# Three tiles turned by DMA instead of TensorE in a mixer and MLP block, with other load order, groups and explicit order lists

## The chip, the cores and the metric

One core of one Trainium2 chip. The metric is the device time of one execution in microseconds (us); a kernel's time is the median of several runs. Engines: TensorE (PE; its weight loads are PEld in the profile), VectorE (DVE), ScalarE (ACT), GpSimd (POOL) and SyncE (SP), which issues nearly all DMAs.

## What is computed

x is 1 x 2048 x 512 in bf16, w1 and w2 are 512 x 512, w3 is 512 x 1792, w4 is 1792 x 512.

```python
h = _gelu(_layernorm(x, axis=-1) @ w1)
c = D // 4
g0 = jnp.pad(h[:, :, 0*c:1*c], ((0, 0), (1, 0), (0, 0)))[:, :S, :]
g1 = jnp.pad(h[:, :, 1*c:2*c], ((0, 0), (0, 1), (0, 0)))[:, 1:, :]
g2 = jnp.pad(h[:, :, 2*c:3*c], ((0, 0), (2, 0), (0, 0)))[:, :S, :]
g3 = jnp.pad(h[:, :, 3*c:   ], ((0, 0), (0, 2), (0, 0)))[:, 2:, :]
hs = jnp.concatenate([g0, g1, g2, g3], axis=-1) @ w2
x1 = x + hs
h2 = _gelu(_layernorm(x1, axis=-1) @ w3) @ w4
return x1 + h2
```

The four quarters of h are shifted along the tokens by 1, -1, 2 and -2 before w2, so a tile of the first residual (x1) needs h of its own tile and of both neighbours.

## The kernel before

The 2048 tokens are 16 tiles of 128. All weights and activations stay in SBUF. A tile passes these steps; t is the tile, q is t in layer 1 and 16 + t in layer 2:

- Load: `dma_x..` and `dma_w..` from SP (line 384 for x, 393 for weights), in the order of `LOADS`. w1, w2 and w4 come in halves a and b, w3 in one piece.
- Statistics: either bn_stats and bn_aggr on DVE (`bnst`, `bnag`, lines 432 and 434), or, for q in `STAT_ACT`, sums and sums of squares on ACT (`sum`, `ssq`, lines 411 and 416) with small DVE steps (`mean`, `msq`, `vpe`). `rstd` is a power on POOL (line 439).
- `norm` on DVE, ACT or POOL by the table `NORM` (lines 461, 470, 473; for ACT and POOL with a small step `nmr` first) writes the normalized tile into one of 16 slots of `xn_buf`.
- The turn, tokens to columns, into `xnT`. On PE: four transposes of 128 x 128 through PSUM and an eviction (`tp` and `ev`, lines 506 and 514; `ty` in the script takes a PSUM pair of the up buffers, `tp` a bank of the other PSUM buffer). Or by DMA: one transposing DMA for the whole tile (line 479), also named `tp`, issued on SP's queue. Which one a tile gets is decided by whether the script names it: tiles 0 to 7 of layer 1 are on PE, the other 24 turns are DMAs.
- `up1` (w1, line 642) in groups of tiles by `GROUPS`: weights are the stationary operand, so a group of n tiles is 16 matmuls of 128 n columns. Tile 0 is done the other way round (`rows`, line 544) and its GELU output is turned by PE (`th`, line 610). GELU on ACT (line 657) writes `hT`.
- `mix` (w2, line 697): four matmuls of 512 columns, one for each shifted quarter; DVE adds x to give x1 (`x1_`, line 713 or 709). The first mix is cut in two parts by which half of w2 comes first.
- Layer 2: statistics, norm and turn again, `up2` (w3, line 642) in blocks of a group, GELU, `down` (w4, line 731): 14 matmuls of 512 columns. DVE adds x1 (`res`, line 739) and SP writes out. The last tile's columns go in pieces of 256, 160 and 96 with the output DMA on ACT's queue.

PE warms up on nine matmuls of zeros while the first x tiles load. Two PSUM banks serve mix, down and some turns, three pairs of banks serve up and the other turns.

PE's order is the order of `SCRIPT`. The order of the other engines is made by a planner in `Program.order` and `place`: each operation has an assumed duration (`dur`), a due time worked back from PE's order, a hand-set bias, and a model of the DMA queue; DMA turns are put among the loads of SP's queue by it. `emit` then writes the instructions in that order with semaphore waits. Every engine works its list in order, and SP's DMAs are issued in order: a DMA turn whose norm is not done holds up those listed after it.

Of the kernel before, what the change touches and what calls it, by code (L numbers as in the profile page):

```python
# [6 lines left out]
P = 128  # L7
# [4 lines left out]
LN_EPS = 1e-5  # L12
ENGINES = ["sp", "act", "pe", "dve", "pool"]

class Op:


    def __init__(self, name, eng, fn, reads, writes, dur, queue):
        self.name, self.eng, self.fn = name, eng, fn
        self.reads, self.writes = list(reads), list(writes)  # L20
        self.dur, self.queue = dur, queue
        self.idx = 0
        self.descs = 8.0
        self.prio = 1e9
        self.first = None

class Program:

    HOP = {"pe": 200.0, "dve": 155.0, "act": 220.0, "pool": 120.0, "sp": 70.0}
    LOOK = {"dve": 300.0, "act": 300.0}
    DUE = 179877.0
    BEGIN = {"sp": 30.0, "act": 150.0, "pe": 400.0, "dve": 150.0, "pool": 450.0}
    ENTRY = 1900.0
    COLD, RESTART = 4300.0, 800.0
    RING = 150.0
    LAG = {"load": 750, "tp": 350}

    def __init__(self):  # L40
        self.ops = []
        self.lines = []

    def add(self, eng, name, fn, reads=(), writes=(), dur=100.0, queue=None):
        op = Op(name, eng, fn, reads, writes, dur, queue)
        op.idx = len(self.ops)
        self.ops.append(op)
        return op

    def line(self, names):  # L50

        self.lines.append(list(names))

    def order(self):
# [25 lines left out]
        order_only = set()  # L80
        for names in self.lines:
            for a, b in zip(names, names[1:]):
                assert named[a].eng == named[b].eng, (a, b)
                order_only.add((named[a].idx, named[b].idx))
        last = None
        pe_pos = 0
        for op in self.ops:
            if op.eng == "pe":
                if last is not None:
                    preds[op.idx].add(last.idx)  # L90
                last = op
                op.prio = pe_pos
                pe_pos += 1
        order_only = {(a, b) for a, b in order_only if a not in preds[b]}
        for a, b in order_only:
            preds[b].add(a)
        succs = [set() for _ in self.ops]
        for i, d in enumerate(preds):
            for j in d:
                succs[j].add(i)  # L100
        left = [len(s) for s in succs]
        stack = [i for i, n in enumerate(left) if n == 0]
        seen = 0
        while stack:
            i = stack.pop()
            seen += 1
            for j in preds[i]:
                if self.ops[j].eng != "pe":
                    self.ops[j].prio = min(self.ops[j].prio, self.ops[i].prio)
                left[j] -= 1  # L110
                if left[j] == 0:
                    stack.append(j)
        assert seen == len(self.ops), "cycle"
        if self.DUE:

# [37 lines left out]
    def place(self, succs, order_only):  # L153
# [9 lines left out]
        fed = {}  # L163
# [745 lines left out]
```

## Time and profile before

| | |
|---|---|
| median of 3 runs | 135.59 us (135.45 to 135.73) |
| span of the profiled execution, first to last instruction | 133.7 us |
| around the span (135.59 - 133.7) | 1.9 us |
| PE busy | 130.6 us, 98% of the span |
| ACT, DVE, POOL busy | 56.0, 50.9, 30.9 us |
| DMA turns | 24, median 2.5 us from issue to landing |
| w3, one load of 1792 KB | 10.9 us from issue to landing |
| PE transposes of x tiles (line 506) | 32 matmuls, 3.4 us busy |

Times in the trace count from the span's start. The chain that ended last follows the work back from the last instruction; a piece of it is a start, a length and what ran. Busy time of PE overlaps between neighbours, since matmuls are pipelined and their ends are modelled; lengths in the chain do not overlap. Landing is the time from a DMA's issue to its last semaphore update. A run of matmuls is sometimes shown with one record fewer than was issued.

### The profile page before, as it was taken

What the parts mean: (1) busy time and instruction counts of PE and PEld (TensorE: products, weight loads), DVE (VectorE), ACT (ScalarE), POOL (GpSimd) and SP (SyncE); (2) the same over time, 40 slices, a digit from 0 to 9 for tenths busy, and PEclk for the clock granted to TensorE, in tenths of its full rate; (3) what the DMA queues carried; (4) which work ended last, traced back from release to release, by engine and by line L of the source; (5) the groups of instructions that cost most, each with busy time, mean ns of one, the idle gap of its engine ahead of it and who ended that gap; (6) DMA issues with size and microseconds to landing.
All of it is one profiled execution on the core that took longest, in us unless ns stands there. A gap on an engine that the chain in (4) does not pass through costs nothing.

```text
span 133.7 us, 2004 instructions
## 1 busy us (share of the span) xinstructions
PE 130.6 (98%) x776; PEld 71.8 (54%) x789; DVE 50.9 (38%) x138; ACT 56.0 (42%) x89; POOL 30.9 (23%) x69
## 2 busy tenths in 40 slices
PE   8999999999999999999999999999999999999994
PEld 3488768874488444444444444444444444444464
DVE  1899998887550830052260003322220000232223
ACT  5699998858657155520025553000006663000000
POOL 2447567696544120012022003100000000000000
PEclk9999999999999999999999999999999999999999
DMA  4999966745442991002211000311111000111112
GB/s 134 329 349 401 237 150 95 83 89 107 98 99 49 295 329 40 0 0 43 77 42 39 0 0 0 78 39 44 39 42 37 0 0 0 39 44 39 39 39 78
DMA packets 21305, 12.19 MB, mean 91 GB/s; under 512 B 13872, under 2 KB 20784, under 8 KB 21296
## 3 DMA queue, kind: packets, MB, share of 16 engines
q1 hardware_dynamic: 20864, 11.93, 32.7%
q10 hardware_dynamic: 432, 0.13, 0.4%
q8 instruction: 6, 0.10, 0.3%
q14 instruction: 3, 0.02, 0.1%
HBM read 6.82 MB, written 2.10 MB: 67 GB/s over the span
## 4 chain that ended last, share of the span: by engine, by line
PE 94%; DMA 2%; DVE 2%; issue 1%; SPq 0%
PE y_ps L642 46%; PE o_ps L731 36%; PE o_ps L697 10%; DMA x_sb<-in_x_dram 2%; PE y_ps L506 1%; DVE st L432 1%; PE y_ps L544 1%; DVE xn_buf L448 0%; DVE xn_buf L461 0%; DVE o_sb L739 0%; PE o_ps L610 0%; DVE mv L434 0%; SPq L894 0%
## 5 line engine op out<-in xcount | busy, mean ns | idle before, releaser
L642 PE MATMUL y_ps<-xnT,w_sb 128*128 128x512 bf16 (+2 forms) x421 | 63.6, 308 | 0.2
L642 PEld LDWEIGHTS y_ps<-xnT,w_sb 128*128 128x128 bf16 x424 | 38.4, 98 | 24.6 <-DVE mv L434 0.2
L731 PE MATMUL o_ps<-w_sb,h2T 128*128 128x512 bf16 (+3 forms) x248 | 48.7, 355 | 0.2
L657 ACT ACTIVATE h2T<-y_ps 128x1024 bf16<-128x1024 f32 (+1 forms) x29 | 28.6, 993 | 47.2 <-PE y_ps L642 47.1
L731 PEld LDWEIGHTS o_ps<-w_sb,h2T 128*128 128x128 bf16 x252 | 23.6, 98 | 25.2
L739 DVE TENSOR_TENSOR o_sb<-o_ps,x_sb 128x512 bf16<-128x512 f32 (+3 forms) x18 | 11.4, 632 | 45.7 <-PE o_ps L731 45.7
L439 POOL TENSOR_TENSOR rstd<-mv,neghalf 128x1 f32<-128x1 f32 x20 | 11.1, 553 | 35.1 <-DVE mv L434 30.1
L697 PE MATMUL o_ps<-w_sb,hT 128*128 128x512 bf16 x58 | 14.8, 379 | 0.3
L432 DVE BATCH_NORM_STATS2 st<-x_sb 128x6 f32<-128x512 bf16 x20 | 13.5, 676 | 2.6 <-DMA x_sb<-in_x_dram 2.5
L713 DVE TENSOR_TENSOR x_sb<-o_ps,x_sb 128x512 bf16<-128x512 f32 x10 | 6.8, 677 | 14.8 <-PE o_ps L697 14.8
L439 POOL TENSOR_TENSOR rstd<-vpe,neghalf 128x1 f32<-128x1 f32 x12 | 6.7, 558 | 15.6 <-DVE vpe L428 15.5
L473 POOL TENSOR_SCALAR xn_buf<-x_sb,rstd,nmr 128x512 bf16<-128x512 bf16 x12 | 9.2, 764 | 1.0 <-DVE nmr L466 0.4
L657 ACT ACTIVATE hT<-y_ps 128x512 bf16<-128x512 f32 (+1 forms) x10 | 8.1, 806 | 3.1 <-PE y_ps L642 2.9
L697 PEld LDWEIGHTS o_ps<-w_sb,hT 128*128 128x128 bf16 x64 | 6.1, 98 | 5.7
L709 DVE SCALAR_TENSOR_TENSOR x_sb<-o_ps,x_sb 128x512 bf16<-128x512 f32 x6 | 4.1, 681 | 12.1 <-PE o_ps L697 12.1
L416 ACT ACTIVATE junk<-x_sb 128x512 bf16<-128x512 bf16 x12 | 7.5, 622 | 2.1 <-DVE x_sb L709 2.0
L461 DVE TENSOR_SCALAR xn_buf<-x_sb,mv,rstd 128x512 bf16<-128x512 bf16 x13 | 6.1, 471 | 2.7 <-POOL rstd L439 2.0
L470 ACT ACTIVATE xn_buf<-x_sb,nmr,rstd 128x512 bf16<-128x512 bf16 x6 | 4.9, 813 | 0.5 <-POOL nmr L466 0.4
L756 PE MATMUL o_ps<-zeros 128*128 128x512 bf16 x9 | 4.0, 631 | 0.4 <-DVE zeros L363 0.4
L411 ACT ACTIVATE junk<-x_sb 128x512 bf16<-128x512 bf16 x6 | 3.7, 624 | 1.2 <-DMA x_sb<-in_x_dram 1.2
L434 DVE BATCH_NORM_AGGREGATE mv<-st 128x2 f32<-128x9 f32 x20 | 3.8, 192 | 0.3
L506 PE MATMUL y_ps<-ident,xn_buf 128*128 128x128 bf16 x32 | 3.4, 236 | 0.2 <-DVE xn_buf L461 0.2
(34 smaller groups left out, 28.7 us busy)
## 6 DMA issues: line engine op xcount, KB each, us to landing
out_dram<-o_sb SPq DMA_DIRECT2D x15, 128.0 KB, 1.7
w_sb<-in_w_dram SPq DMA_DIRECT2D x1, 1792.0 KB, 10.9
w_sb<-in_w_dram SPq DMA_DIRECT2D x2, 896.0 KB, 6.2
x_sb<-in_x_dram SPq DMA_DIRECT2D x4, 256.0 KB, 3.6
w_sb<-in_w_dram SPq DMA_DIRECT2D x4, 256.0 KB, 4.3
x_sb<-in_x_dram SPq DMA_DIRECT2D x5, 128.0 KB, 4.5
x_sb<-in_x_dram SPq DMA_DIRECT2D x1, 384.0 KB, 5.7
xnT<-xn_buf SPq DMA_TRANSPOSE x24, 2.5
```

The source lines that it names most:

```text
L416: (lambda d: (lambda e: e.activation(d, src, ACT_F.Square, accum_out=sums[:, q, 1:2])))(junk[:, b, :]),
L432: pg.add("dve", f"bnst{q}", lambda e: e.bn_stats(st9[:, q, 0:6], src), reads=rs, writes=[(("st", q), 0)], dur=605)
L439: lambda e: e.tensor_tensor(col(rstd), var, neghalf[:], ALU.pow),
L461: lambda e: e.tensor_scalar(dst, src, mv[:, q, 0:1], rstd[:, q : q + 1], ALU.subtract, ALU.mult),
L470: f = lambda e: e.activation(dst, src, ACT_F.Identity, bias=nmr[:, q : q + 1], scale=rstd[:, q : q + 1])
L473: f = lambda e: e.tensor_scalar(dst, src, rstd[:, q : q + 1], nmr[:, q : q + 1], ALU.mult, ALU.add)
L642: ins = e.matmul(y_ps[:, p, W * i : W * (i + 1)], wsb[:, dc, P * fc : P * (fc + 1)], src[:, dc, P * t0 : P * t0 + W], start=(dc == 0), sto ...
L657: (lambda d, s: (lambda e: e.activation(d, s, ACT_F.Gelu_apprx_tanh)))(dst, ysrc),
L697: ins = e.matmul(dst, hT[:, j, c0 : c0 + P], w2_sb[:, j, :], start=(j == order[0]), stop=(j == order[-1]))
L713: f = lambda e: e.tensor_tensor(x1_sb[:, t, :], dst, x_sb[:, t, :], ALU.add)
L731: ins = e.matmul(dst, h2T[:, fc, P * t : P * (t + 1)], w4_sb[:, fc, cs], start=(fc == 0), stop=(fc == FC - 1))
L739: (lambda d, c: (lambda e: e.tensor_tensor(o_sb[:, oi, c], d, x1_sb[:, t, c], ALU.add)))(dst, cs),
```

## The change

- Tiles 5, 6 and 7 of layer 1 are no longer in the script as turns, so they become transposing DMAs on SP's queue (tp5, tp6, tp7). PE turns tiles 0 to 4; tile 3 goes through the other PSUM buffer.
- Layer 1's groups: tiles 0 to 7 one by one (5 and 6 were a pair), then 2, 2 and 4. Layer 2's groups: 2, 4, 4, 4, 2 instead of 2, 2, 4, 4, 4.
- Loads: x5 alone between the halves of w1; x4 alone; x6 and x7 together, ahead of w2a; x8 and x9 together; w3 in four pieces of 448 KB (s, p, q, r), with tp5 between the second and the third; x10 to x15 and w4 on SP's queue after ten more DMA turns.
- The script names up2 blocks one at a time and mixes them with mix, down and up1.
- The planner is gone. `ORDER` lists every operation of SP, ACT, DVE and POOL; `order` only merges these lists and PE's script.
- Other tables of who does which statistics, norm and eviction: two tiles of layer 1 have their statistics on ACT instead of six; the eviction of tile 0's turned GELU output goes from DVE to ACT, tile 1's turn is evicted by ACT alone.

```diff
-GROUPS = {1: (1, 1, 1, 1, 1, 2, 1, 2, 2, 4), 2: (2, 2, 4, 4, 4)}
+GROUPS = {1: (1, 1, 1, 1, 1, 1, 1, 1, 2, 2, 4), 2: (2, 4, 4, 4, 2)}
-NORM = {5: "act", 6: "pool", 7: "act", 9: "pool", 10: "pool", 11: "act", 12: "act", 15: "pool", 18: "act", 19: "pool", 20: "act", 21: "pool", 23: "pool", 25: "pool", 26: "pool", 28: "pool", 30: "pool", 31: "pool"}
+NORM = {4: "act", 6: "act", 7: "pool", 10: "pool", 11: "act", 12: "pool", 14: "act", 16: "pool", 17: "pool", 18: "act", 20: "act", 21: "pool", 24: "act", 26: "pool", 27: "pool", 28: "pool", 29: "pool", 30: "act", 31: "act"}
-EVAC = {1: "both", 2: "dve", 4: "dve", 5: "dve", 6: "both", 7: "dve", 8: "dve", 9: "dve", ...
+EVAC = {0: "act", 1: "act", 2: "both", 3: "dve", 4: "both"}
-STAT_ACT = (0, 5, 7, 9, 10, 12, 19, 21, 23, 24, 25, 31)
+STAT_ACT = (0, 9, 18, 19, 23, 25, 26, 31)
...
-HEV = {0: "dve", 1: "dve", 2: "dve", 3: "dve", 4: "dve", 5: "dve", 6: "dve"}
-BIAS = {"bnag16": -989.166, "nmr10": 207.118, "rstd14": 756.261, "rstd5": 886.138, ...
+HEV = {0: "act"}
 LOADS = """
-x0-1 x2 tp2 w1a w1b x3 x4-5 w2b w2a tp5 x6 tp6 x7 x8-10 tp4 w3 x12-13 tp0 x11 tp17 x14-15 tp26 tp5 w4a tp3
-w4b
+x0-1 x2 w1b x5 w1a x3 w2a x4 x6-7 w2b w3p w3s w3r w3q x10-11 w4a w4b x8-9 x15 x12 x14 x13
 """
+W2FIRST = "b"
 SCRIPT = """
-warm:9 sa:0 sb:0 ty:1 ra:0 rb:0 ty:2 up1:1 th:0 up1:2 mix:0 ty:3 mix:1 ty:4 up1:3 ty:5 up1:4 ty:6 mix:2
-up1:5 ty:7 mix:3 up1:6 mix:5 mix:4 up2:0 up1:7 mix:6 up1:8 mix:7-8 up1:9 mix:10 mix:9 up2:1 mix:13 mix:11
-up2:2 mix:14 down:2 down:1 down:0 mix:12 up2:3 mix:15 down:3 down:5 down:7 down:4 down:6 down:10 up2:4
-down:8 down:11 down:9 down:12-15
+warm:9 sa:0 sb:0 ty:1 ra:0 rb:0 ty:2 up1:1.0 th:0 up1:2.0 tp:3 mix:0 up1:3.0 ty:4 mix:1 mix:2 up1:4.0 up1:5.0
+mix:3 mix:4 up1:6.0 up1:7.0 mix:5 mix:6 up2:0.0 up2:0.4 up2:0.8 up1:8.0 up2:0.12 up2:1.0 up2:1.2 mix:8 mix:7
+up2:1.4 up2:1.6 up2:1.8 up2:1.10 down:0 up1:9.0 up2:1.12 mix:9 up1:10.0 down:4 up1:10.2 up2:2.0 mix:11 mix:14
+...
+down:10 down:14 down:9 down:12 down:11 down:13 down:15
 """
+ORDER = {
+    "sp": """
+dma_x0 dma_x2 dma_w1a dma_x5 dma_w1b dma_x3 dma_x4 dma_w2b dma_x6 dma_w2a dma_x8 dma_w3s dma_w3p tp5 dma_w3q
+dma_w3r tp6 tp7 tp16 tp17 tp9 tp8 tp20 tp18 tp19 tp21 dma_x15 dma_x10 dma_x12 dma_x13 dma_x14 dma_w4b dma_w4a
+tp11 tp10 tp22 tp12 tp14 tp15 tp13 out_dma0_0 tp23 tp24 tp25 tp28 tp31 tp26 tp29 tp30 tp27 out_dma1_0
+...
+    "act": """
+warm_gelu sum0 ssq0 ev0_0 ev0_1 ev1 gelur0 ev2act gelu1_1_0 evh0 gelu1_2_0 norm4 ssq9 gelu1_3_0 ev4act norm6
+sum9 gelu1_4_0 gelu1_5_0 ssq18 ssq19 gelu1_6_0 gelu1_7_0 norm20 norm18 gelu2_0_0 gelu2_0_4 gelu2_0_8 gelu1_8_0
+...
+    "dve": """
+zeros bnst1 bnag1 norm0_0 norm0_1 bnst2 norm1 bnag2 msq0 bnst5 vpe0 norm2 bnag5 bnst3 ev2dve bnag3 norm5 bnst4
+norm3 bnag4 bnst6 ev3 bnag6 x1_0 nmr6 bnst7 ev4dve bnst16 bnag7 bnag16 bnst8 x1_1 bnst17 nmr16 bnag17 x1_2
+mean18 msq18 msq9 x1_3 vpe18 vpe9 mean19 bnag8 msq19 x1_4 vpe19 norm9 bnst20 norm8 bnag20 x1_5 nmr20 x1_6
+bnst21 bnst22 bnag21 bnag22 norm22 norm19 bnst15 bnst11 bnst13 bnag11 x1_8 bnst24 bnag13 bnag15 bnag24 bnst10
+...
+    "pool": """
+trip0 trip1 neghalf ident0 epsc pad0 ident1 pad1 rstd1 rstd2 rstd0 rstd5 rstd3 rstd4 nmr4 rstd6 rstd7 rstd16
+nmr7 norm7 norm16 rstd17 nmr17 norm17 rstd9 rstd18 rstd8 rstd20 nmr18 rstd22 rstd19 rstd21 nmr21 norm21 rstd11
+...
+}
...
-        def mm_up(layer, g):
+        def mm_up(layer, g, only=None):
...
-            for f0 in range(0, nfc, per):
+            for f0 in range(0, nfc, per) if only is None else (only,):
```

In `Program.order` the whole planning is replaced by this merge (an operation is taken when all that it depends on has been taken):

```diff
+        lists = {e: [named[n] for n in ORDER[e].split()] for e in ENGINES if e != "pe"}
+        lists["pe"] = [op for op in self.ops if op.eng == "pe"]
...
+        while len(out) < len(self.ops):
+            heads = [lists[e][at[e]] for e in ENGINES if at[e] < len(lists[e])]
+            heads = [op for op in heads if preds[op.idx] <= done]
+            op = min(heads, key=lambda op: (op.name not in AHEAD, ENGINES.index(op.eng)))
+            at[op.eng] += 1
+            done.add(op.idx)
+            out.append(op)
```

The names of a DMA are those of its first tile: dma_x6 loads tiles 6 and 7, dma_x8 tiles 8 and 9, dma_x10 tiles 10 and 11, dma_x0 tiles 0 and 1. The junk buffers of the ACT sums are now given out in the order of ACT's list.

## The prediction

> **What bounds the kernel now.** I read the page's busy shares first, then the chain that ended last, then TensorE's (PE's) timeline around the edit, and last the DMA queue. PE is busy 98% of the span at full granted clock, and the chain is 94% PE:
>
> ```profile
> PE 130.6 (98%) x776; PEld 71.8 (54%) x789; DVE 50.9 (38%) x138; ACT 56.0 (42%) x89; POOL 30.9 (23%) x69
> PEclk9999999999999999999999999999999999999999
> ...
> PE 94%; DMA 2%; DVE 2%; issue 1%; SPq 0%
> ```
>
> In the chain in order of time, PE runs without a hole from 5.12 us (first turn of tile 1) to 131.94 us; the pieces of 0.05 called issue stand where a matmul's record is missing (x3 where four were issued), and each pair fills the time of four. So the kernel is a sum of PE pieces, and whatever takes a piece out counts, unless PE must then wait for something that it hardly waits for now. The pieces that price the change:
>
> ```profile
> 6.70 0.89 PE y_ps L642 x16
> ...
> 9.58 0.22 PE y_ps L506 x4
> 9.80 0.86 PE o_ps L697 x4
> ...
> 13.98 1.75 PE y_ps L642 x16
> ```
>
> One tile of up1 costs 0.89, a group of two tiles 1.75, a turned tile (four transposes) 0.22, a mix 0.86. The chain counts from modelled ends and stands 0.16 behind the timeline of starts (up1 of tile 1: 6.70 there, 6.54 here), so against landings I use starts.
>
> The DMA queue, by narrow windows of its issues, in this order: the three-tile x load (x8 to x10), w3 in one piece, x11, then the first two DMA turns of layer 2 (tp16, tp17), with KB and us from issue to landing:
>
> ```profile
> x_sb<-in_x_dram SPq DMA_DIRECT2D x1, 384.0 KB, 5.7
> w_sb<-in_w_dram SPq DMA_DIRECT2D x1, 1792.0 KB, 10.9
> x_sb<-in_x_dram SPq DMA_DIRECT2D x1, 128.0 KB, 10.8
> xnT<-xn_buf SPq DMA_TRANSPOSE x1, 3.4
> xnT<-xn_buf SPq DMA_TRANSPOSE x1, 2.5
> ```
>
> Issued at 5.06, 5.54, 6.68, 14.67 and 15.99, they land at 10.8, 16.4, 17.5, 18.05 and 18.5. So a DMA turn that is ready early lands about 0.55 behind the last load queued ahead of it, and the next turn 0.45 later.
>
> **The change, part by part.**
>
> *Turns leave PE.* Tiles 5, 6, 7 lose 3 x 0.22 = 0.66 of PE. Tiles 5 and 6 were one up1 group (1.75) and become two of one tile (2 x 0.89 = 1.78): +0.03. Net -0.63. All other PE work is the same in count: turns of 0 to 4, mixes, sixteen tiles of up1, 112 up2 matmuls of 256 columns and 168 of 512, all of down, and the same 256/160/96 tail. The new mixture of up2 blocks with down moves pieces and removes none. If nothing waited: 135.59 - 0.63 = 134.96. The profile's span is 133.7; the three timed runs have a median of 135.59, so 1.9 lie around the span, and I put the difference on the median.
>
> *When PE wants the turned tiles.* From the start of up1 of tile 1 (6.54) the new script has before tile 5: up1 of 1 and 2, turns of h0 and tile 3, mix 0, up1 of 3, turn of 4, mixes 1 and 2, up1 of 4: 4 x 0.89 + 3 x 0.22 + 3 x 0.86 = 6.80. PE reaches up1 of tile 5 at 13.34; after 0.89 and two mixes, tile 6 at 15.95; tile 7 at 16.84; up2 at 19.45. In the kernel before, tile 6 needed no landing at all here.
>
> *When they land.* tp5, tp6, tp7 stand in SP's queue behind loads. Ahead of tp5 are x0 to x9, w1, w2 and two quarters of w3: 1280 + 1024 + 896 = 3200 KB. Before, 2432 KB (through x10) had landed at 10.8 and 4224 KB (through w3) at 16.4, or 3.1 us per 1000 KB. So the loads ahead of tp5 land at 13.2 and tp5 at 13.75, while its issue is early: x5 lands between w1a and w1b (4.7 and 5.5 before), and bn_stats, rstd and norm of tile 5 are done near 7.6. SP then waits at tp5 for norm5 with w3q, w3r and tp6 queued behind it; their issues at about 8.9 cost nothing, as w3s and w3p keep the engines busy till past 12. tp6 stands behind 4096 KB (16.0) and tp5 (0.45): 16.45, plus 0.55, 17.0. tp7 follows at 17.45, tp16 and tp17 at 17.9 or later, before up2 wants them. tp6's own norm (ACT, about 12.5) is not late.
>
> So PE waits for tp5 until 13.8 and for tp6 until 17.05; both waits together are 17.05 - 15.95 = 1.1, since the first is inside the second. Tile 7 comes 0.89 later, after tp7.
>
> *How sure tp6 is.* At 14.1 the page's instruction queue takes one DMA engine away in the same stretch (window 14 to 15, 6.6% of 16 engine-us, so 1.05 us of one engine):
>
> ```profile
> q1 hardware_dynamic: 295, 0.32, 88.4%
> q8 instruction: 1, 0.02, 6.6%
> ```
>
> w3 lands only when its last engine is done, so part of its 16.4 is this fetch. PE's instructions reach the same count near tile 5 in the new order, so I leave the fetch in; without it tp6 would land near 16.0 and PE wait 0.1. From above, DMA turns stop the stream around them: with tp16 under way and one load's last part late, the queue moved almost nothing for 0.7 us:
>
> ```profile
> 15.80:16.50 0.70, 0.70 (x7) 1.00 0.84 180
> 16.50:17.20 0.70, 0.70 (x12) 1.00 1.18 41
> 17.20:17.90 0.70, 0.70 (x12) 1.00 0.99 190
> ```
>
> (Last two columns: DMA share and GB/s.) If tp5 does that with half of w3 behind it, tp6 lands at 17.7 and PE waits 1.8. I take the middle, 17.0, since its row (tp16 behind w3 and x11) is the nearest: the same queue, the same fetch, 384 KB less ahead.
>
> A turn in the trace moves its 128 KB at 180 to 190 GB/s, where w3 moves at 405 to 412 (windows 11 to 13). The Trainium skill (Advanced Engine Details and Errata, X-Bar Transpose (TRN2)) has transposing DMAs as fast as regular ones, 350 to 400 GB/s; by that tp5 would cost the queue about 0.35 instead of 0.45 and the sum would fall by 0.1; the trace disagrees and decides.
>
> The trace's DMA turn takes 2.5 us to land on a free queue, PE's 0.22 of stream and an eviction. The Trainium skill (VectorE: DVE Perf Modes, Rules for kernel authors) speaks against this change: a 128x128 transpose belongs on TensorE if PSUM as its destination is acceptable, and on the DMA crossbar otherwise. Its table has 390 ns against 1309 ns for each; by it the three tiles would save PE 12 x 0.39 = 4.7, an estimate that the chain's 0.66 refutes, as transposes are pipelined.
>
> *The head.* x5's 128 KB ahead of w1b move its landing from 5.5 to 5.85; the second half of tile 0's product starts near 5.9, not 5.74 (+0.15). bn_stats of x5 (0.60) goes ahead of vpe0 and so of rstd0 and the first GELU; the eviction of h0 goes from DVE (0.41) to ACT (0.60) behind another GELU; tile 1's goes whole to ACT. w2a, now behind x6 and x7, lands where x7 did, at 9.1 (4.59 + 4.5), and mix 0's second half wants it near 9.2. I expect 0 to 0.3 from these, and all of it lies inside the 1.1 that PE waits for tp6. If that wait is gone, it shows.
>
> *The first block of layer 2.* x10 to x15 and w4 load after tp21. From the end of mix 6: x1 (0.8 with the hop), two bn_stats (1.2), two aggregates (0.3), rstd22 and rstd19 (1.1), norm19 with hops (0.6), tp19's issue (1.27), tp21 to landing (2.5): 7.75. PE has 3.5 blocks of up2 and tile pair 8-9 for that time: 4.5 x 1.75 = 7.86. That is a tie; a POOL norm that overlaps a DVE norm stretched the latter from 0.41 to 0.80 at 25.5 before, so I bound it by 0 and 0.4 and take 0.05. The late x loads add waits on DVE: at bn_stats of tile 15, near 30, it waits with x1 of tile 8 queued behind it, but that tile's mix ends only near 33, so nobody waits. Later landings have room: w4 near 37 against its use near 40, tp13 0.5, tp30 0.8.
>
> *The rest at nothing.* ACT, DVE and POOL exchange statistics and norms (four fewer ACT pairs in layer 1 and others), under PE work. At 42% and 38% busy they hide it past 30 us; the price without that cover is one norm, 0.4 to 0.8.
>
> Sum: -0.63 + 1.1 + 0.05 = +0.5, or 136.1.
>
> **Rivals.**
> - *The turns are in time* (faster). One mechanism: at up1 of tile 6 tp6 has landed, because the fetch falls on another moment or the quarters land sooner than one w3 did. It decides below about 16.2 for tp6; at zero wait the time is 134.96 plus up to 0.2 of the head, so 135.0 to 135.2. For it: quarters let each engine end sooner, 16.0 without the fetch. Against it: tp16's row, and three parts must all go well.
> - *Balance*: tp6 at 16.3 to 16.8, wait 0.35 to 0.85, 135.3 to 135.85.
> - *tp5 stops the queue* (slower still): tp6 at 17.7, 136.8. For it the 41 GB/s row; against it, that stop had an engine late by over a microsecond.
>
> **How the numbers follow.** Forecast (tp6 16.8 to 17.5) 0.47; in time 0.24; balance 0.14; stop 0.15. A measurement of this kernel tells about 0.2% (0.27 us) from no change. Faster is the second case, 0.24; same 0.14; slower 0.47 + 0.15 = 0.62. The range has to take in most of the first rival and most of the stop: 135.1 to 136.9. The forecast's own range is 135.9 to 136.6.
>
> **What would show it.** Right: 20 PE transposes of x tiles instead of 32; PE idle before a one-tile up1, ended by the DMA xnT<-xn_buf, 1.1 in all between 13 and 17.2; the first 256-column matmul starting near 20.6 (19.27 before, 19.45 without waits); the same chain from there but for at most 0.2 at the first 512-column block. Wrong: no such idle time (the first rival), idle time of 0.5 or more past 30 us, or a tp6 that lands before 16.2.

## The result, and the profile after

Four runs of the changed kernel have a median of 137.43 us (137.03 to 138.33) beside 135.52 us of the kernel before in the same job; the ratio is 1.0153 with a 95% interval of 1.0115 to 1.0190. A second job gave 137.65 us and 1.0155 (1.0131 to 1.0178). So it is slower by 2.1 us, where 0.5 was forecast. The profiled execution took 137.61 us with a span of 135.9. Times of the changed kernel's relatives below spread over up to 3.6 us from run to run, and they ran on several chips; so each is told by its ratio to the runs of before in its own job, and a difference of less than some 0.5 us between two of them is left to the traces. Runs over 1.5% above the fastest of their kernel are left out of the ratios, while the medians take in all runs.

From the page, the lines that answer to those of before: busy time, the granted clock, and the chain by engine.

```profile
PE 131.3 (97%) x781; PEld 70.9 (52%) x793; DVE 50.0 (37%) x137; ACT 53.9 (40%) x78; POOL 28.4 (21%) x64
PEclk9999999999999999999999999999999999999999
...
PE 84%; DMA 6%; ACT 3%; DVE 2%; issue 2%; SPq 1%; POOL 1%; ACTq 0%
```

The clock is full as before. The chain, 94% PE before, has lost ten points to DMA and the vector engines: PE waits for them now. Where, PE's timeline shows (start, length, instruction; in brackets the idle time ahead of it and what ended it):

```profile
6.83 0.60 PE L381 MATMUL y_ps<-w_sb,xnT 128*128 128x512 bf16 x2 [0.22 <-DMA w_sb<-in_w_dram]
...
7.49 1.06 PE L477 MATMUL y_ps<-xnT,w_sb 128*128 128x128 bf16 x16
...
17.66 1.96 PE L477 MATMUL y_ps<-xnT,w_sb 128*128 128x128 bf16 x32 [0.34 <-DMA xnT<-xn_buf]
19.51 1.92 PE L531 MATMUL o_ps<-w_sb,hT 128*128 128x512 bf16 x8
21.26 8.02 PE L477 MATMUL y_ps<-xnT,w_sb 128*128 128x256 bf16 x72
30.04 1.24 PE L477 MATMUL y_ps<-xnT,w_sb 128*128 128x512 bf16 x5 [0.76 <-ACT h2T L492]
```

In the kernel before, PE has no idle time in brackets on these stretches; up1 of tile 1 (7.49 above) and the 256-column groups of up2 (21.26) stand there as

```profile
6.54 1.06 PE L642 MATMUL y_ps<-xnT,w_sb 128*128 128x128 bf16 x16
...
19.27 8.02 PE L642 MATMUL y_ps<-xnT,w_sb 128*128 128x256 bf16 x72
```

Four places in the changed kernel: the second half of w1 (6.83); tile 6's turn (17.66: the x32 are up1 of tiles 6 and 7); the first 512-column group of up2 (30.04); and, too short for a bracket in this profile, the group of tiles 12 to 15 at 49.4 and the one of tiles 30 and 31 at 79.5. At 30.04 the first matmul's record is missing: 15 steps of 0.216 lead from 30.04 to the next mix at 33.27, where 16 were issued, so PE began at 29.82, 0.13 after tile 21's turn landed at 29.69. The GELU named as releaser (ended at 29.96) comes from the missing record.

The second profile has all 793 of PE's matmuls on record, so the starts can be added up (what a matmul's start lies behind its predecessor's beyond the usual 56 ns for 128 columns, 109 for 256 and 216 for 512 is counted as waiting): tile 1's first turn starts 0.09 later than before, then 0.12 and 0.79 around tile 0's product (w1b), 0.50 for tile 6, 0.68 for tile 21, 0.48 for the group of tile 13, and 0.23 in five small pieces. That is 2.89; less 12 transposes at 56 ns, 0.67, it is 2.22, and PE's last matmul starts at 133.92 instead of 131.72, 2.20 later. Between these two profiles nothing is missing from the sum. Against an ordinary run of before, part of the agreement is luck: in the second job before's 16 runs have spans of 133.7 to 134.7 us with a median of 134.1, and the profile used here, at 133.7, is a quick one. The changed kernel's four have a median of 135.9, so 1.8 of the 2.2 us lie inside the span. The other 0.4 lie outside it (1.63 to 1.88 us of the time, 1.30 to 1.38 before), where the profile shows no instruction.

The chain that ended last, in order of time, explains tile 6 otherwise (start, length, what):

```profile
1.57 4.51 DMA x_sb<-in_x_dram
...
13.56 4.05 DMA xnT<-xn_buf
...
17.66 1.96 PE y_ps L477 x32
```

It goes back from the landing to the turn's issue, from there through ACT's and VectorE's norms to x5's load, and so names x5 as the cause. The experiments show that the 4.05 us are not a fixed time from the issue: issued at 12.89, 13.03 or 13.64, the turn landed at 17.43, 17.63 and 17.20 (walls, mix_walls, x5_back). The queue sets the landing.

What the DMA queue did while tile 6's turn was in flight, in columns of length, busy time of PE, PEld, DVE, ACT, POOL, granted clock, DMA share and GB/s:

```profile
14.00:15.00 1.00, 1.00 (x22) 1.00 (x20) 0.97 (x2) 0.48 (x3) 0.90 (x3) 1.00 1.01 376
15.00:15.60 0.60, 0.52 (x10) 0.47 (x9) 0.60 (x4) 0.30 (x2) 0.60 (x2) 1.00 2.95 179
15.60:16.20 0.60, 0.58 (x3) 0.19 (x2) 0.56 (x3) 0.60 (x2) 0.60 (x2) 1.00 0.03 3
16.20:16.80 0.60, 0.60 (x5) 0.29 (x4) 0.56 (x4) 0.58 (x2) 0.52 (x2) 1.00 0.30 19
16.80:17.40 0.60, 0.52 (x3) 0.03 (x1) 0.60 (x6) 0.17 (x1) 0.47 (x2) 1.00 1.02 211
```

For 1.2 us the queue moves next to nothing. From 14.95 to 16.02 us one DMA engine is away on an instruction fetch of 16 KB. In the kernel before the same fetch (14.10 to 15.15) fell on w3's one load, and the other fifteen engines went on:

```profile
14.10:15.20 1.10, 1.10 (x12) 0.98 (x11) 1.07 (x5) 1.10 (x3) 0.70 (x2) 1.00 0.87 299
```

So a load by itself loses one engine's share to a fetch, and a DMA turn in flight loses the whole fetch and more. Tile 6's turn took 4.06 us from issue to landing where 2.5 is the median, but loads stood ahead of it, so that length alone proves little. Better is the load between the two turns: w3's last quarter landed 2.62 us behind the third (16.97 and 14.35), where quarters are otherwise about 1.15 apart, so the fetch of 1.07 us cost 1.47.

The traces of all kernels here, taken together, bear this out. 179 turns had neither a fetch nor a load or store in flight beside them, and every one took 2.40 to 2.56 us. Of the turns without a load or store beside them, each that took more than 2.6 had an instruction fetch in its flight; where one of 16 KB began 0.9 to 2.1 us after the issue, the turn took 3.7 to 4.4. And in x5_back (below) the fetch came at another time, though no edit aimed at it: 11.57 to 12.69 us, with tile 5's turn in flight and tile 6's not yet issued. There the delay moved with it: w3's second quarter, right ahead of tile 5's turn, landed at 13.65 instead of 12.7, the queue moved 9 GB/s from 12.69 to 13.30, and the last quarter came 1.13 us behind the third.

The same page of after has two more such places. A fetch at 24.33 us (1.06 long) lengthened tile 20's turn to 4.1 us, and one at 45.28 (1.08) tile 14's to 4.1. While a turn is in flight so long SP issues the next one and then stands: tile 19's turn was issued at 25.85 though its norm had ended at 25.21, and tile 13's at 46.82 though its norm had ended at 46.14. Those are the waits at 30 and 49 us.

### The profile page after: what moved, and what is told of

Read it like the earlier page. It is cut to its first block, busy times and chain, and to the rows that moved or that the text cites. A ratio compares the mean times of both kernels' runs of the same rounds, so it can differ in the third digit from the quotient of the medians.

```text
span 135.9 us, 1999 instructions
## 1 busy us (share of the span) xinstructions
PE 131.3 (97%) x781; PEld 70.9 (52%) x793; DVE 50.0 (37%) x137; ACT 53.9 (40%) x78; POOL 28.4 (21%) x64
## 4 chain that ended last, share of the span: by engine, by line
PE 84%; DMA 6%; ACT 3%; DVE 2%; issue 2%; SPq 1%; POOL 1%; ACTq 0%
PE y_ps L477 42%; PE o_ps L565 36%; PE o_ps L531 7%; DMA x_sb<-in_x_dram 3%; DMA xnT<-xn_buf 3%; ACT xn_buf L308 1%; ACT hT L492 1%; DVE xn_buf L299 1%; SPq L224 1%; DVE st L271 1%; ACT junk L255 0%; POOL rstd L278 0%; ACT h2T L492 0%; SPq L233 0%; DVE mv L273 0%
## 5 line engine op out<-in xcount | busy, mean ns | idle before, releaser
L565 PE MATMUL o_ps<-w_sb,h2T 128*128 128x512 bf16 (+3 forms) x249 | 49.6, 355 | 0.2
L271 DVE BATCH_NORM_STATS2 st<-x_sb 128x6 f32<-128x512 bf16 x24 | 16.3, 681 | 10.2 <-DMA x_sb<-in_x_dram 10.1
L278 POOL TENSOR_TENSOR rstd<-mv,neghalf 128x1 f32<-128x1 f32 x24 | 13.1, 548 | 30.0 <-DVE mv L273 29.0
L308 ACT ACTIVATE xn_buf<-x_sb,nmr,rstd 128x512 bf16<-128x512 bf16 x9 | 7.2, 810 | 5.2 <-POOL nmr L304 2.6
L311 POOL TENSOR_SCALAR xn_buf<-x_sb,rstd,nmr 128x512 bf16<-128x512 bf16 x10 | 7.6, 766 | 1.5 <-DVE nmr L304 0.8
L278 POOL TENSOR_TENSOR rstd<-vpe,neghalf 128x1 f32<-128x1 f32 x8 | 4.5, 565 | 11.4 <-DVE vpe L267 11.3
L299 DVE TENSOR_SCALAR xn_buf<-x_sb,mv,rstd 128x512 bf16<-128x512 bf16 x12 | 4.8, 408 | 3.2 <-POOL rstd L278 3.1
L255 ACT ACTIVATE junk<-x_sb 128x512 bf16<-128x512 bf16 x8 | 5.0, 623 | 1.4 <-DVE x_sb L543 1.4
L304 POOL TENSOR_SCALAR nmr<-mv,rstd 128x1 f32<-128x1 f32 x10 | 2.6, 261 | 0.8
L590 PEld LDWEIGHTS o_ps<-zeros 128*128 128x128 bf16 x9 | 1.2, 142 | 2.4 <-issue 1.9
```

Of the source, the lines that this page charges most:

```text
L271: pg.add("dve", f"bnst{q}", lambda e: e.bn_stats(st9[:, q, 0:6], src), reads=rs, writes=[(("st", q), 0)])
L278: lambda e: e.tensor_tensor(col(rstd), var, neghalf[:], ALU.pow),
L299: lambda e: e.tensor_scalar(dst, src, mv[:, q, 0:1], rstd[:, q : q + 1], ALU.subtract, ALU.mult),
L308: f = lambda e: e.activation(dst, src, ACT_F.Identity, bias=nmr[:, q : q + 1], scale=rstd[:, q : q + 1])
L311: f = lambda e: e.tensor_scalar(dst, src, rstd[:, q : q + 1], nmr[:, q : q + 1], ALU.mult, ALU.add)
L565: ins = e.matmul(dst, h2T[:, fc, P * t : P * (t + 1)], w4_sb[:, fc, cs], start=(fc == 0), stop=(fc == FC - 1))
```

## The experiments

Every order list is written out in the changed kernel, so a part is undone by moving names. For the kernel before, its planner's orders were written out in the same form, which leaves its instructions as they were. The table gives, for each kernel, the ratio to before with its interval, and from its profile: when tile 6's turn landed, when the first 256-column matmul of up2 started (19.27 before), and the waits past that for tile 21, for the group of tile 13 and for that of tile 30.

| kernel | median us | ratio (95%) | tp6 lands | first 256 | waits 21 / 13 / 30 |
|---|---|---|---|---|---|
| changed | 137.43 | 1.0153 (1.0115 to 1.0190) | 17.62 | 21.26 | 0.70 / 0.10 / 0.29 |
| after_again | 137.65 | 1.0155 (1.0131 to 1.0178) | 17.54 | 21.19 | 0.68 / 0.48 / 0 |
| pe_turns | 137.03 | 1.0122 (1.0066 to 1.0177) | PE | 21.31 | 0.29 / 0.54 / 0 |
| mix_first | 137.45 | 1.0119 (1.0082 to 1.0157) | 17.53 | 21.18 | 0 / 0.78 / 0.16 |
| pe_mix | 137.43 | 1.0116 (1.0058 to 1.0175) | PE | 21.77 | 0 / 0.93 / 0 |
| x5_back | 137.71 | 1.0143 (1.0100 to 1.0187) | 17.20 | 20.99 | 0.96 / 0.31 / 0 |
| walls | 137.24 | 1.0118 (1.0089 to 1.0147) | 17.43 | 21.08 | 0 / 0 / 0 |
| mix_walls | 136.62 | 1.0111 (1.0077 to 1.0145) | 17.63 | 21.28 | 0 / 0 / 0 |
| pe_mix_walls | 136.79 | 1.0096 (1.0077 to 1.0114) | PE | 21.12 | 0 / 0 / 0 |
| x_mix_walls | 137.17 | 1.0125 (1.0107 to 1.0142) | 18.30 | 21.95 | 0 / 0 / 0 |
| tp5_behind | 138.61 | 1.0141 (1.0099 to 1.0184) | 17.05 | 21.86 | 0 / 0.10 / 0 |
| pe5 | 136.85 | 1.0093 (1.0075 to 1.0111) | 17.17 | 22.18 | 0 / 0 / 0 |
| pe5_w2a | 136.83 | 1.0089 (1.0068 to 1.0110) | 16.56 | 21.94 | 0 / 0 / 0 |
| head_loads | 136.86 | 1.0106 (1.0079 to 1.0133) | PE | 21.88 | 0 / 0 / 0 |
| bx5 | 135.62 | 1.0007 (0.9991 to 1.0023) | PE | 20.01 | none |
| bx_w2a | 136.03 | 1.0037 (1.0015 to 1.0059) | PE | 20.07 | none |
| bx567 | 140.88 | 1.0272 (1.0213 to 1.0331) | 17.87 | 26.08 | none |

### First four: the head and the wait for tile 21

**pe_turns.** Tiles 5 to 7 back on PE.

```diff
-mix:1 mix:2 up1:4.0 up1:5.0 mix:3 mix:4 up1:6.0
+mix:1 ty:5 mix:2 up1:4.0 up1:5.0 mix:3 ty:6 mix:4 ty:7 up1:6.0
-EVAC = {0: "act", 1: "act", 2: "both", 3: "dve", 4: "both"}
+EVAC = {0: "act", 1: "act", 2: "both", 3: "dve", 4: "both", 5: "dve", 6: "dve", 7: "dve"}
 sp: -tp5 -tp6 -tp7     dve: +ev5 after x1_1, +ev6 after x1_3, +ev7 before x1_4
```

> The changed kernel with tiles 5, 6 and 7 turned by TensorE again, as before the change (12 turns in four banks each, evictions on VectorE); loads, groups and all other orders stay. Theory A, that the landing of tile 6's DMA turn (17.62 us) sets when TensorE gets through the head: no wait for a DMA before tile 7's first projection, the first 256-column matmul of group 0 near 20.5 us instead of 21.26 although TensorE does 0.66 us more turns. But the wait for tile 21's turn in front of the second 256-column matmul group grows by what the head wins (0.70 to about 1.3 us), so the time moves by no more than 0.3 us: 137.1 to 137.4. Theory B, that the head is late only by x5 standing ahead of the second half of w1 (up-projection of tile 1 at 7.49 instead of 6.54 us): the first 256-column matmul is at 21.2 us or later, and the time is higher by up to 0.66 us: 137.4 to 138.0.

Measured: 137.03, 1.0122. The first 256-column matmul starts at 21.31, as theory B has it (21.2 or later) and not at theory A's 20.5, with no DMA in the way. The time is below both, 137.1 and 137.4 to 138.0. PE's line through the head:

```profile
13.32 2.18 PE L477 MATMUL y_ps<-xnT,w_sb 128*128 128x128 bf16 x32
15.34 1.03 PE L531 MATMUL o_ps<-w_sb,hT 128*128 128x512 bf16 x4
16.20 0.39 PE L344 MATMUL y_ps<-ident,xn_buf 128*128 128x128 bf16 x4
...
21.31 0.92 PE L477 MATMUL y_ps<-xnT,w_sb 128*128 128x256 bf16 x7
```

Up1 of tiles 4 and 5 takes 2.02 from start to start instead of 1.83, as tile 5's eviction on DVE is late, and so on in small pieces of 0.07 to 0.22. Theory A as worded falls: take tile 6's DMA turn away and PE arrives no sooner, for it has 0.67 of turns again and waits for their evictions.

**mix_first.** Two mixes ahead of the groups that need tile 21.

```diff
-up2:0.0 up2:0.4 up2:0.8 up1:8.0 up2:0.12 up2:1.0 up2:1.2 mix:8 mix:7
+up2:0.0 up2:0.4 up1:8.0 up2:0.8 up2:0.12 mix:8 mix:7 up2:1.0 up2:1.2
 act: -gelu2_0_8 gelu1_8_0   +gelu1_8_0 gelu2_0_8
```

> The changed kernel with TensorE's order altered between 21 and 31 us alone: tile 8's projection one matmul group earlier, and mixes 8 and 7 ahead of the two matmul groups that need tile 21's turn; ScalarE's two gelus follow that order. Theory A, that the 0.70 us before the second 256-column group are a wait for tile 21's turn (landed 29.69): it is hidden by work that has its inputs, and the time falls by 0.5 to 0.8 us, to 136.6 to 136.9. Rival: TensorE waits in another place for VectorE's sums or ScalarE's gelus, which the mixes moved ahead now ask for earlier, and the time falls by less than 0.3 us.

Measured: 137.45, no change by the medians; by the ratios (1.0119 against 1.0153 and 1.0155) it is some 0.45 us less, with intervals that overlap, and below the 0.5 to 0.8 of theory A. The wait at 30 us is gone from the profile, as theory A has it, and the time with it has gone into one at 49.3:

```profile
47.84 0.81 PE L526 MATMUL o_ps<-w_sb,hT 128*128 128x512 bf16 x3
49.27 1.02 PE L472 MATMUL y_ps<-xnT,w_sb 128*128 128x512 bf16 x4 [0.62 <-issue]
```

The second row is the group of tiles 12 to 15; its last turn (tile 13's) landed at 49.18 here and at 49.28, 49.35, 49.92 and 49.46 in the other four profiles so far. It does not come with PE: SP's queue sets it.

**pe_mix.** Both edits.

> The two edits together: tiles 5 to 7 turned by TensorE, and the mixes moved ahead of the groups that need tile 21. Theory A: with tile 21's wait hidden, the head's gain reaches the end: 0.3 to 0.8 us below the kernel with the mixes moved alone, 136.0 to 136.4. Theory B (head late by x5 and the second half of w1 alone): 0.3 to 0.7 us above the kernel with the mixes moved alone, for the turns that TensorE does again.

Measured: 137.43, outside both theories. In the head PE waited 0.68 for w2a (landed 10.21) and at 50 us 0.93 for tile 13.

**x5_back.** x5 behind w1b and x3, with VectorE's order as before in its first steps.

```diff
-dma_w1a dma_x5 dma_w1b dma_x3      +dma_w1a dma_w1b dma_x3 dma_x5
 dve: -msq0 bnst5 vpe0 norm2 bnag5 bnst3    +msq0 vpe0 norm2 bnst3 ev2dve bnag3 bnst5 bnag5
```

> The changed kernel with x5's load put back behind the second half of w1 and x3, and VectorE's square root of tile 0's variance and norm 2 ahead of tile 5's statistics, as before the change; all DMA turns stay. Theory A: the up-projection of tile 1 starts near 6.6 us instead of 7.49, but tile 6's turn still lands at 17 us or later, so TensorE waits about 1 us more for it and the time moves by less than 0.3 us: 137.1 to 137.7. Theory B: the head's 0.9 us reach the end, 136.5 to 136.7.

Measured: 137.71, as theory A has it and not B. w1b landed at 6.24 instead of 6.78 and up1 of tile 1 began at 7.08 (expected 6.6), tile 6's turn still landed at 17.20, and what was won went into 0.96 for tile 21. x5's place is not what costs in this kernel.

### The late waits

The theory formed from these (C): two late turns are walls that give back whatever is won ahead of them. **walls** moves only orders past 39 us:

```diff
 sp:
-tp11 tp10 tp22 tp12 tp14 tp15 tp13 out_dma0_0 tp23 tp24 tp25 tp28 tp31 tp26 tp29 tp30 tp27
+tp11 tp10 tp13 tp12 tp14 tp15 tp22 out_dma0_0 tp23 tp24 tp25 tp30 tp27 tp31 tp29 tp28 tp26
 dve: norm13 from behind res0_0 to behind bnag14
```

> The changed kernel with two stretches of SP's order and one VectorE norm moved, all past 39 us: norm 13 goes ahead of norms 15 and 23, tile 13's turn from last to first of the four turns that tiles 12 to 15 need (tile 22's goes behind them), and the turns of tiles 30 and 27, whose norms end at 63.8 and 63.2 us, go ahead of those of 31, 29, 28 and 26. Theory C: TensorE waits at two places past the head, for tile 13's turn near 49.3 us and for tile 30's near 79.3, and these two waits alone go (0.10 and 0.29 us in the changed kernel's profile); the 0.7 us for tile 21 stay: 0.3 to 0.4 us less, 137.0 to 137.2. Rival D, that those waits only follow lateness that came before them: no change, 137.4.

> The same edit on the kernel with the mixes ahead of the groups that need tile 21. Theory C: there the 0.70 us won at 30 us were lost again at 49.3 us, where tile 13's turn lands at 49.2 us whatever TensorE did before (waits of 0.10, 0.54, 0.78, 0.93 and 0.31 us in the five profiles, landings of 49.28, 49.35, 49.18, 49.92 and 49.46). With the turns reordered the last of the four lands near 47.9 and TensorE comes at 48.5: the waits of 0.78 and 0.16 us go and the time falls by 0.8 to 1.0 us, to 136.1 to 136.5. Rival D: tile 15's turn, now last, is held up in the same way by the turn ahead of it, which is in flight during an instruction fetch; it lands at 49.2 and the time stays at 137.2 to 137.5.

> The same edit on the kernel with tiles 5 to 7 turned by TensorE and the mixes moved. Theory C: its wait of 0.93 us at 50 us goes: 0.7 to 1.0 us less, 136.3 to 136.7 if the head is as late as in that profile (first 256-column matmul at 21.8 us), 135.9 to 136.2 if it is as in the kernel with the turns alone (21.3). Against the kernel with the DMA turns and the same edits this says what three DMA turns in the head are worth: theory A, that tile 6's landing sets the head, wants it 0 to 0.4 us faster; a gain from the DMA turns shows it up to 0.6 us slower.

> The same edit, the mixes moved, and x5's load behind the second half of w1 as before the change; the turns of tiles 5 to 7 stay on DMA. Theory A: tile 6's landing near 17.2 us sets the head in spite of the earlier start, so the time is within 0.3 us of the kernel with x5 ahead and the same edits: 136.0 to 136.4. If x5's place is what costs, 0.5 to 0.9 us less: 135.5 to 135.8, which is level with the kernel before the change.

Measured: 137.24, 136.62, 136.79 and 137.17. In all four profiles both waits are gone. The last of the four turns landed at 47.11, 47.50, 48.23 and 48.60, tile 30's at 65.3 to 66.2 instead of 79, and mix_walls has PE from its first up2 matmul on without a hole, which theory C wants and rival D does not:

```profile
17.68 1.96 PE L472 MATMUL y_ps<-xnT,w_sb 128*128 128x128 bf16 x32 [0.78 <-DMA xnT<-xn_buf]
19.52 1.92 PE L526 MATMUL o_ps<-w_sb,hT 128*128 128x512 bf16 x8
21.28 8.02 PE L472 MATMUL y_ps<-xnT,w_sb 128*128 128x256 bf16 x72
29.14 1.89 PE L526 MATMUL o_ps<-w_sb,hT 128*128 128x512 bf16 x8
30.86 10.52 PE L472 MATMUL y_ps<-xnT,w_sb 128*128 128x512 bf16 x48
```

The gain in time is smaller than expected: 0.2 us for walls, 0.8 for mix_walls, by medians, and by the ratios 1.0111 against 1.0154, about 0.6 us with intervals that overlap. Against the profile before, PE's last matmul still starts 1.1 us late (132.85). Of that, with the 12 transposes taken off, 0.16 is tile 1's later turn, 0.50 w1b, 0.94 tile 6 and 0.22 small pieces: the head. pe_mix_walls says what three DMA turns in that head are worth: 1.0096 against 1.0111, nothing that can be told. x_mix_walls, by 1.0125, is no faster than mix_walls with x5 ahead; its w2a landed at 10.35 and PE waited for it, and again for tile 6's turn, which landed at 18.30:

```profile
10.40 0.61 PE L526 MATMUL o_ps<-w_sb,hT 128*128 128x512 bf16 x2 [0.63 <-DMA w_sb<-in_w_dram]
...
18.35 0.84 PE L472 MATMUL y_ps<-xnT,w_sb 128*128 128x128 bf16 x12 [0.91 <-DMA xnT<-xn_buf]
```

### Is it the turn in the stream?

Theory E: a DMA turn makes all 16 DMA engines wait for the slowest. For it: in after w3's third quarter landed within 0.06 us on all 16 engines (14.29 to 14.35) behind tile 5's turn, where in pe_turns, with no turn, it came between 12.72 and 14.22. And the last quarter landed at 16.5 to 17.7 us in six profiles with the turn ahead of it, and at 15.30, 16.50 and 14.91 in three without.

**tp5_behind** (on mix_walls) puts tile 5's turn behind all of w3; **pe5** (on mix_walls) turns tile 5 on PE.

```diff
 tp5_behind:
-dma_w3p tp5 dma_w3q dma_w3r tp6      +dma_w3p dma_w3q dma_w3r tp5 tp6
-mix:2 up1:4.0 up1:5.0 mix:3 mix:4 up1:6.0 up1:7.0 mix:5
+up1:4.0 mix:2 mix:3 up1:5.0 up1:6.0 mix:4 up1:7.0 mix:5
 act: -norm6 sum9 gelu1_4_0   +norm6 gelu1_4_0 sum9
 pe5:
-mix:1 mix:2     +mix:1 ty:5 mix:2       sp: -tp5      dve: +ev5 after x1_1
```

> On the kernel with the mixes and the late turns moved (136.62 us): tile 5's turn goes from between w3's quarters to behind the last of them, so that no turn stands in the load stream; TensorE takes tile 4's projection one mix earlier and tile 5's one mix later to make up for it. Theory E: a DMA turn in the stream makes all 16 DMA engines wait for the slowest of them (with the turn, w3's last quarter landed at 16.5 to 17.7 us in six profiles, on 15 or 16 engines at once; without it at 14.9 to 16.5 us in three, spread over 1.3 us or more), so moving it behind brings the last quarter to 15.5 us or earlier, tile 5's turn to about 16 and tile 6's to about 16.5 instead of 17.6; TensorE waits about 0.7 us for tile 5 and no more: 0.2 to 0.5 us less than that kernel, 136.1 to 136.4. Rival: the queue is late whatever stands in it, tile 5's turn lands at 17.2 or later, and the time rises by over 1 us.

> On the same kernel tile 5 is turned by TensorE again (0.22 us more of it) and tiles 6 and 7 by DMA. By theory E the quarters of w3 land by 15.5 us, tile 6's turn by 16.5, when TensorE wants it near 17: the wait of 0.94 us goes, the sum is 0.7 us less, 135.8 to 136.1. Rival (tile 6's turn lands near 17.5 whatever is ahead): 0 to 0.3 us less.

Measured: 138.61 and 136.85. For theory E the landings go its way, but both times lie outside what it gave: tp5_behind's rose, as the rival had it, by 0.3% against mix_walls by the ratios, with overlapping intervals, and pe5's came out 0.2% lower, within its rival's 0 to 0.3 us. In tp5_behind the last quarter landed at 15.88 instead of 16.98, tile 5's turn at 16.41 and tile 6's at 17.05, 0.6 sooner; but PE waits longer for tile 5 than it did for tile 6, and then anew, for tile 8's turn, which the fetch of that stretch (24.52, 1.13 long) caught in flight: issued at 21.71, landed at 26.43. One more row of that trace narrows theory E: w3's last quarter landed on all 16 engines within 0.06 us (15.82 to 15.88) there too, though no turn stands ahead of it; one is queued right behind. In after the second quarter, right ahead of tile 5's turn, landed within 0.10 us (12.62 to 12.72), and in pe_turns, with no turn near, between 11.59 and 13.09. So it is a turn next to a load, ahead or behind, that goes with all engines ending together.

```profile
16.46 1.96 PE L472 MATMUL y_ps<-xnT,w_sb 128*128 128x128 bf16 x32 [1.20 <-DMA xnT<-xn_buf]
...
26.47 4.54 PE L472 MATMUL y_ps<-xnT,w_sb 128*128 128x256 bf16 x40 [0.95 <-DMA xnT<-xn_buf]
```

In pe5 fifteen engines had done the last quarter of w3 by 14.54 us and the sixteenth, some 1.4 us behind the others since w2's load at 9.36, at 16.49; tile 6's turn, issued at 13.96, landed on all 16 between 16.99 and 17.17. That is the waiting for the slowest in one case. PE did not wait for tile 6 any more, but 0.85 for w2a (landed 10.78) and 0.44 for tile 17.

### Which loads, and what else is in the head

**bx5** and **bx_w2a** do one part each alone to the kernel before, **bx567** the turns alone.

```diff
 bx5:     -dma_w1a dma_w1b dma_x3 dma_x4 (tiles 4 and 5)   +dma_w1a dma_x5 dma_w1b dma_x3 dma_x4
 bx_w2a:  -dma_w2b dma_w2a dma_x6 dma_x7    +dma_w2b dma_x6 dma_x7 dma_w2a
 bx567:   -ty:5 ty:6 ty:7 and their evictions    +tp5 tp6 tp7 on SP, right behind dma_w3
```

> The kernel before with one part of the change alone: x5 loads by itself between the halves of w1, x4 by itself behind x3; every order on the engines is that of before. My sum priced this at 0.35 us of w1's second half and 0.15 us of TensorE, hidden only by a later wait, which this kernel does not have: 135.6 to 135.9. The changed kernel's profile says more: w1's second half landed at 6.0 to 6.8 us in the kernels with x5 ahead of it (5.5 before): up to 0.9 us, 136.4.

> The kernel before with one part of the change alone: the first half of w2 loads behind x6 and x7 instead of ahead of them. Mix 0's second half wants it near 9.2 us; it landed at 8.43 before and at 9.36 to 10.78 in the ten profiles that have it behind. Theory F, that this half is late by 0 to 0.85 us with nothing to hide it: 135.6 to 136.4, with one wait of TensorE for the w2 load near 9.5. Rival (it lands by 9.2, as my prediction had it): 135.5.

> The kernel before with another part alone: tiles 5, 6 and 7 are turned by DMA, issued right behind w3, which stays one load; loads, groups and every other order are those of before. Tiles 5 and 6 are one group there and wanted near 13.3 us; w3 landed at 16.5, so the turns land at 17.0 to 18 and TensorE waits 3.5 to 4.5 us, less 0.66 for the turns, and what is late of it next: 138.3 to 139.5. A rival, that so long a wait is made up elsewhere, has no row: TensorE waited for nothing past 5.1 us before.

Measured: 135.62, 136.03 and 140.88. x5 alone costs 0.1 us (1.0007, interval -0.1 to 0.3 us); its profile has PE wait 0.66 for the second half of w1 all the same (landed 6.57), and its last matmul start 0.73 later than in before's profile, which is another sign that this one profile of before is a quick one. w2a behind x6 and x7 alone costs 0.5 (1.0037, 0.2 to 0.8 us): it landed at 9.72, and in its profile mix 0 takes 1.16 from start to start instead of 0.86:

```profile
9.05 1.32 PE L528 MATMUL o_ps<-w_sb,hT 128*128 128x512 bf16 x4
10.21 0.39 PE L341 MATMUL y_ps<-ident,xn_buf 128*128 128x128 bf16 x4
```

bx567: the turns landed at 17.39, 17.87 and 18.35, about as expected, and PE waited 3.93 us for them. Then came something that no theory had: after that wait PE ran at half its clock for 5.9 us (granted clock in the last but two columns).

```profile
18.00 3.57 PE L471 MATMUL y_ps<-xnT,w_sb 128*128 128x256 bf16 x16 [3.93 <-DMA xnT<-xn_buf]
```

```profile
18.00:20.00 2.00, 2.00 (x10) 1.41 (x11) 0.00 (x0) 0.00 (x0) 0.00 (x0) 0.50 0.91 249
20.00:22.00 2.00, 2.00 (x10) 1.20 (x9) 0.00 (x0) 0.39 (x1) 0.00 (x0) 0.50 0.52 91
22.00:23.50 1.50, 1.50 (x8) 0.72 (x6) 0.18 (x1) 1.24 (x3) 0.00 (x0) 0.50 0.83 229
23.50:24.00 0.50, 0.50 (x8) 0.50 (x7) 0.50 (x3) 0.00 (x0) 0.00 (x0) 0.64 0.00 0
24.00:26.00 2.00, 2.00 (x18) 1.14 (x16) 1.80 (x9) 1.45 (x4) 0.88 (x2) 1.00 0.00 0
```

At half clock, 5.9 us do the work of 2.95, so this accounts for some 2.9 of the 3.5 us between the profiled run, 141.85, and the one of the four that had a full mean clock, 138.31, inside the expectation. Whether PE's wait was shorter in that one is not on record.

**pe5_w2a** (pe5 with w2a ahead of x6, ev3 ahead of tile 6's statistics) and **head_loads** (pe_mix_walls with x5 behind w1b and w2a ahead of x6, VectorE's first 20 us fitted) undo load orders on top.

> The kernel with tiles 6 and 7 alone turned by DMA behind w3 and the mixes and late turns moved (136.85 us; its profile waited 0.85 us for the first half of w2), with that half loading ahead of x6 and x7 and VectorE's eviction of tile 3 ahead of tile 6's statistics. Theory F: no wait for w2, 0.2 to 0.8 us less, 136.1 to 136.6. Rival: VectorE, which now gets x6 later, holds up tiles 5 and 6 by as much, 136.8.

> The kernel with all of layer 1 turned by TensorE and the mixes and late turns moved (136.79 us), with x5 behind the second half of w1, the first half of w2 ahead of x6 and x7, and VectorE's order in the head fitted to it. No load of the head then stands otherwise than before but for w3's quarters. If the load order is what is left of the loss: 135.5 to 135.9, level with the kernel before. If the sharing among the vector engines is (24 statistics on VectorE instead of 20, its evictions late): waits for evictions and mixes between 13 and 20 us of 0.5 us and more, 136.2 to 136.6.

Measured: 136.83 and 136.86; neither won anything. w2a was in time in both (9.12, 8.83). In its place PE waited for evictions of the turns that VectorE, now busy with statistics of x6 that came later, did late. head_loads:

```profile
14.39 1.07 PE L472 MATMUL y_ps<-xnT,w_sb 128*128 128x128 bf16 x16 [0.55 <-DVE xnT L347]
...
19.04 1.07 PE L472 MATMUL y_ps<-xnT,w_sb 128*128 128x128 bf16 x16 [0.30 <-DVE xnT L347]
```

These rows bear out the second of the two expectations for head_loads, sharing among the vector engines, at 136.86 rather than 136.2 to 136.6.

**after_again.**

> The changed kernel once more, without an edit, for a second profile. Expected as in the first: 136.9 to 137.7 us, tile 6's turn landed between 17.2 and 17.7, a wait before the first 512-column group near 30 us and one each before the groups that need tiles 13 and 30.

Measured: 137.65, tile 6's turn at 17.54, waits at the same places but for tile 30's. The first profile was typical, its early loads too (x5 5.90 and 6.08, w1b 6.75 and 6.78, w2a 9.54 and 9.71).

No kernel here is faster than before: the best of those with the change's groups, pe5_w2a at 1.0089, is slower than before, and bx5 is level with it.

## Why the prediction was wrong, by its own steps

- *Turns leave PE, -0.63.* Right: 0.67 by the starts.
- *When PE wants the turned tiles.* Right. In the second profile tile 6's up1 starts at 17.59; without the 1.64 that PE had by then waited or begun late, 15.95, the forecast figure.
- *When they land.* This step failed first. tp5 came at 13.21 (13.75 forecast), early, because the two quarters ahead of it took 2.55 us per 1000 KB (10.43 to 12.72) and not 3.1, a figure that had the fetch in it; but tp6 came at 17.62 and 17.54 (17.0) and tp7 at 18.02 (17.45). The fetch was in the forecast at 1.0 us (16.0 without it), as a load's, and the turn at 0.55 behind the last quarter. Beside a turn the fetch held up the whole queue, and the last quarter came 2.62 us behind the third instead of 1.15: 1.47 for the fetch, and then 0.65 for the turn. These two, 0.47 and 0.1, are the missing 0.55 to 0.6. The third rival, tp5 stops the queue, tp6 at 17.7, has the right number, and I gave it 0.15, on the row with 41 GB/s; in part that is luck, for tp5 by itself did not stop the queue (399 GB/s from 13.20 to 14.35), and the stop came at the fetch. I then took that row's cause for one late engine that would not come again.
- *The head, all covered by the wait for tp6.* Right as a mechanism: x5_back starts up1 of tile 1 0.4 us sooner, and tile 6's turn sets the pace all the same. Its size, 0 to 0.3, was wrong: PE had lost about 1.1 there by 17 us, nearly all of it at w1b (landed 6.78, forecast 5.85), which counts once the turns are given another place. Of that x5's place is only a part: w1b landed 0.68 to 0.78 us behind w1a in the six profiles without x5 between them and 1.07 to 1.76 behind it in the twelve with it, so x5's share is 0.3 to 1.0. The rest is w1a itself, which stands behind the same loads in every kernel and landed between 4.74 and 5.69; before's profile, from which the forecast was made, is the earliest. w2a (9.71, forecast 9.1) came just in time in this profile and 0.3 to 0.85 late in five others. bx5 and bx_w2a price the two alone, where nothing hides them: 0.1 and 0.5 us.
- *The first block of layer 2, a tie, 0.05.* Second failure, 0.68 to 0.70. From the end of mix 6 (21.26) to tile 21's landing (29.69) it took 8.43 us, forecast 7.75; to norm 19's end it took the 4.0 that were forecast, and 0.64 is SP standing ahead of tile 19's issue while tile 20's turn was held up (25.21 to 25.85). The trace of before shows it: its turn of tile 11, with a fetch of 1.48 us in flight, took 4.2 us to land, and tile 13's followed tile 12's issue by 2.3 us instead of 1.3. I had listed SP's issue at 1.27 and no more.
- *Room: tp13 0.5, tp30 0.8.* Third failure: 0.10 and 0.29 in one profile, 0.48 and 0 in the other. The first is the same mechanism (tile 14's turn, a fetch at 45.3), the second an order: tile 30's turn stood behind four whose norms end 5 to 9 us later. Room that is smaller than one held-up turn (1.5 us) was no room.
- So the sum: +0.5 forecast; 0.6 for the landing, 0.65 for tile 21 and 0.4 to 0.5 for the late groups make 2.2, which is what the profiles of before and after differ by (1.8 inside the span against an ordinary run of before). What I had named as a sign of error, idle time of 0.5 or more past 30 us, is there at 30.04.
- *The Trainium skill.* VectorE: DVE Perf Modes, Rules for kernel authors, prefers TensorE for a 128x128 transpose where PSUM will do as its destination; here three tiles turned by one or by the other gave the same time (1.0096 and 1.0111, pe_mix_walls and mix_walls). Advanced Engine Details and Errata, X-Bar Transpose (TRN2), has 350 to 400 GB/s; while tile 6's turn moved its own bytes the queue shows 211, and in the two stretches ahead of that 19 and 3.

What stays open: no edit moves the fetch by itself. That it holds a turn up rests on the 179 turns without one, on the turns with one, and on x5_back, where it fell on another turn (in the heads of these kernels it began between 11.57 and 15.63 us). Why the queue stands longer than the fetch lasts (1.47 us for 1.07) the traces do not say. And the 1.2 us that are left with the late waits removed are, by the profiles, several waits of the head (w1b, w2a, tile 6 or the evictions) that take each other's place, whose shares these runs do not part; some of it lies outside the span (1.29 to 1.84 us there, 1.3 to 1.4 in the kernel before).

## What to carry to other kernels

Price a DMA turn by the worst that the trace shows for one, not the median, and look what else used a DMA engine when that happened: here a load by itself went on at 299 GB/s beside a fetch, beside a turn the queue stood, and SP's list behind it stands too. When a wait is taken away, look for the next landing that does not depend on it: here 0.7 us won at 30 us were lost at 49. And list each SP queue by when its norms end, not by tile: two stretches of SP's order and one norm, all past 39 us, removed both late waits.

## What the runs showed of the hardware

- After 3.93 us without a matmul PE's granted clock was 0.50 until 5.9 us past the wait's end; the record of the clock fell at 17.04, 3.0 us after the last matmul had ended (14.08). After waits of 1.2 us and less it stayed at 1.00. The Trainium skill, TensorE: Matmul & The Clock Gate, Part 1, has half the clock after an idle window of about 3.4 us; the rows agree roughly, with a fall after 3.0 us and none after 1.2.
- A DMA turn with neither a fetch nor a load beside it took 2.40 to 2.56 us from issue to landing (179 turns). With a fetch of 16 KB (0.9 to 1.6 us on one DMA engine) that began 0.9 to 2.1 us after its issue, and no load, it took 3.7 to 4.4. In tile 6's turn in after the queue was down to 3 GB/s in between.
- A 448 KB load right behind a turn landed on all 16 engines within 0.06 us (after, 14.29 to 14.35), one right ahead of a turn within 0.06 and 0.10 us (tp5_behind, after); without a turn near the engines were 1.5 us apart (pe_turns).
